# Output stores of whole 128-row tiles in a linear-attention and SwiGLU kernel on one Trainium2 core

## The chip, the cores and the metric

The kernel runs on one core of one Trainium2 chip. Its time is the device time of an execution in microseconds (us). Five engines work side by side, each through its own list of instructions: PE multiplies matrices, DVE and ACT work on vectors and read PE's results from PSUM, POOL and SP mostly issue transfers here. The data are moved by the 16 DMA engines of the core. An instruction waits on semaphores for what it needs, and everything behind it in the same list waits with it.

## The reference

The kernel computes a linear attention and feeds its result to a feed-forward block. The part that matters, cut:

```
q, k, v: [8, 8, 576, 64]          # batch, heads, positions, head size
phi(x) = concat(relu(x) * cos(theta), relu(x) * sin(theta))   # theta = pi/2 * position / 576
kv  = einsum('bhsf,bhsd->bhfd', phi(k), v);  z = sum over s of phi(k)
num = einsum('bhsf,bhfd->bhsd', phi(q), kv)
den = einsum('bhsf,bhf->bhs', phi(q), z) + 1e-6
x   = (num / den) transposed to [8 * 576, 8 * 64]             # 4608 tokens of 512
g   = x @ w_gate;  val = x @ w_val                            # [512, 1536] each
out = (g * sigmoid(g) * val) @ w_out                          # [4608, 512] in float32
```

The output has 4608 x 512 float32 values, 9.4 MB.

## The kernel before, in words

**Tiles.** The positions of a batch are dealt to partitions so that position p of 64 partitions holds 9 tokens in a row: `out_v = out.rearrange("(b p c) f -> b c p f", p=SH, c=NC)` with SH = 64 and NC = 9. So there are 8 x 9 = 72 chunks of 64 tokens; the tokens of a chunk lie 9 rows apart in the output. A tile is two chunks in order, 128 partitions: chunk 2t on partitions 0 to 63, chunk 2t + 1 on 64 to 127. There are 36 tiles. Where 2t is the last chunk of a batch (2t % 9 is 8), the tile straddles two batches. Four tiles (512 tokens) are a token group, tg 0 to 8.

**Stages.** The attention of a batch makes its tiles of x, SP transposes them with DMA (L749 writes xT; L852 transposes the features phi(q), named phit, for the products L789). The matmuls of gate and value (L990), and of the output (L1155), are done for most groups with seven products of half-size blocks in place of eight (a Winograd scheme); the sums that these need are made by DVE (L963 for xT, L1106 for the hidden values). Group 0, and a part of group 1, use plain matmuls (L917, L1065, L1275). In `out_jobs` the four blocks of a group's output are called e11, e12, e21 and e22: first or second pair of tiles, first or second 256 columns. They are evicted from the PSUM banks to a buffer `ob` by ACT (L632) and DVE (L636, L1212). In the last group the pieces are evicted tile by tile, into memory that r_q had held, so the profile shows them as r_q.

**Stores.** `store_jobs` (L1118) stores a tile as two transfers of 64 rows of 512 columns (L1124): from POOL for groups 1 to 6, from SP for group 0 and for group 7's first two tiles. The last group has stores of its own: `store_two_jobs` (L1248) stores 64 rows of two tiles and 256 columns in one transfer, the first half of the rows from SP, the second from ACT (L1253); `store_tile_jobs` (L1258) does the same for one tile (L1262).

**The order of the work.** Each piece of work is a job with the engines that can do it, the jobs that it comes after, and the rooms (PSUM banks, a pair of `ob`) that it gets and puts back. The jobs are numbered as they are made, and written out in an order given by a table of numbers, ORDER, with the room that a job takes behind a colon. Times in the Job calls (`tail`, `dma`, the number beside the engine) are estimates for a planner that made such a table; with a table given they change nothing in the program.

Of the kernel before, what the change touches and what calls it, by code (L numbers as in the profile page):

```python
# [18 lines left out]
def kernel(  # L19
# [10 lines left out]
    nc = tc.nc  # L30
# [4 lines left out]
    SH = 64  # L35
    NC = S // SH
# [1081 lines left out]
    def store_jobs(t, after, put, queues, cols=slice(0, d_model)):  # L1118
        for e in range(2):
            q_ = queues[e]  # L1120

            def fn(j, e=e):
                idx = 2 * t + e
                {"POOL": nc.gpsimd, "SP": nc.sync, "ACT": nc.scalar}[j.eng].dma_start(  # L1124
                    out=out_v[idx // NC, idx % NC][:, cols], in_=ob_of(t)[e * SH:(e + 1) * SH, cols])
            Job({q_: 535 if q_ == "POOL" else 610}, fn, after=after, put=put, tail=1500.0, dma=(1450.0, 480.0))
# [3 lines left out]
    def ob_of(t):  # L1130
        return pair_of(t // 2)[:, t % 2]

    def pair_of(p):
        return (ob_last if obs[p].kind == "last ob" else ob_all)[:, obs[p].at[0]]

    def out_jobs(tg, key):
# [68 lines left out]
        if last:  # L1205
            store_two_jobs(t0, slice(0, HD), [e11], ("SP", "ACT"))
# [7 lines left out]
        if last:  # L1214
            store_two_jobs(t0 + 2, slice(HD, d_model), e22, ("SP", "ACT"))
# [6 lines left out]
        if last:  # L1222
            for n in range(2):
                store_tile_jobs(t0 + 2, n, slice(0, HD), [e21[n]])
        else:
            for t in (t0 + 2, t0 + 3):
                store_jobs(t, e22 + e21, [rooms[1]], ("POOL", "POOL"))
# [8 lines left out]
        if last:  # L1236
            for n in range(2):
                store_tile_jobs(t0, n, slice(HD, d_model), [e12[n]])
        else:
            for t in (t0, t0 + 1):  # L1240
                store_jobs(t, [e11] + e12, [rooms[0]], ("SP", "SP") if tg == NTG - 2 else ("POOL", "POOL"))
# [5 lines left out]

    def store_two_jobs(t, cols, after, queues):  # L1248
        for e in range(2):
            def fn(j, e=e):  # L1250
                (b, c), (b1, _) = divmod(2 * t + e, NC), divmod(2 * t + 2 + e, NC)
                assert b == b1
                {"SP": nc.sync, "ACT": nc.scalar}[j.eng].dma_start(  # L1253
                    out=out_v[b, c:c + 3:2, :, cols].rearrange("c p f -> p c f"),
                    in_=pair_of(t // 2)[e * SH:(e + 1) * SH, :, cols])
            Job({queues[e]: 660}, fn, after=after, tail=1300.0, dma=(700.0, 560.0))

    def store_tile_jobs(t, i, cols, after, queues=("SP", "ACT")):  # L1258
        for e in range(2):
            def fn(j, e=e):  # L1260
                b, c = divmod(2 * (t + i) + e, NC)
                {"SP": nc.sync, "ACT": nc.scalar}[j.eng].dma_start(  # L1262
                    out=out_v[b, c][:, cols], in_=pair_of(t // 2)[e * SH:(e + 1) * SH, i, cols])
            Job({queues[e]: 620}, fn, after=after, tail=1300.0, dma=(700.0, 280.0))
# [36 lines left out]
    for lo, hi in ((0, 2), (2, 4)):  # L1301
        def fn(j, lo=lo, hi=hi):
            o = raws[1, "k"][:, lo:hi]
            relu_on(j.eng, o, o)
# [118 lines left out]
    for tg in range(1, NTG):  # L1423
# [43 lines left out]
        6:7 4:6 12:1 8:0 10:5 16:3 20:4 29 5:8 9:7 13:0 17:1 1:3 376 7 187 28 191 11 186 188 189 31 30 24:7 18:2 26:3  # L1467
        22:6 21:6 25:2 33 32 2:7 67:0 34:45 14:1 70a 36a 35a 38a 37a 3 27 380 19 68v 69 15 23 71 0 41:2 44 40:0 43
        72:340 84:7 78:561 39:1 42 73 74 75:3 85a 79 86 80 87v 81:2 88 76:3 77 45 101:7 89:560 95:341 47 90 96 377
        102a 378 91 92:3 97 48 82:5 93:6 55:1 83 94 98:0 192 193 109 190 103 110 113 381 114 46 99:1 51:3 52 49  # L1470
# [105 lines left out]
```

## Time and profile before

| | before |
|---|---|
| median of 3 runs (lowest to highest) | 299.13 us (298.21 to 299.59) |
| the profiled execution's own time | 298.66 us |
| span of the profiled execution | 296.8 us |
| mean granted clock of PE | 0.996 |
| PE busy, matmuls | 290.1 us (98%), 3292 |
| DVE, ACT, POOL busy | 252.9, 199.1, 69.1 us |
| bytes moved by the DMA queues | 40.90 MB, 138 GB/s |
| stores from POOL, SP, ACT | 52, 18, 6 |

The span goes from the first instruction to the last; the time is taken around it, 1.86 us more in the profiled execution. The stores from SP are 12 halves of 128 KB (8 for group 0, 4 for group 7), and in the last group 2 of two tiles and 4 of one; those from ACT are 2 and 4 of the last group. Instructions that issue a transfer are marked SPq, ACTq and POOLq, and are not counted as busy time. A line "DMA packets" counts the packets of all transfers by size; a store of 64 rows of 512 columns has 64 packets of 2 KB, one of 256 columns packets of 1 KB. The chain is followed back from the last instruction, at each step to what released it.

### The profile page before, as it was taken

The page shows a single profiled execution, that of the slowest core. Times are in us where ns is not written, and L with a number is a line of the kernel's source. Part 1 is how long each engine was busy: PE and PEld are TensorE (multiplying, and loading weights), DVE is VectorE, ACT ScalarE, POOL GpSimd, SP SyncE. Part 2 cuts the span into 40 slices and gives each one's busy share as a digit, 9 for nine tenths or more (in the row PEclk, how much of TensorE's full clock was granted, in tenths as well). Part 3 has the DMA queues.
Part 4 walks back from the last instruction along what each step waited for, and adds up shares of the span by engine and source line. Part 5 has one row for each costly group of instructions (what it writes and reads, how often), then busy time and mean ns, then how long its engine had stood idle before and what let it go on. Part 6 is the DMA issues. An engine that isn't in the chain of part 4 may idle for free.

```text
span 296.8 us, 8157 instructions
## 1 busy us (share of the span) xinstructions
PE 290.1 (98%) x3292; PEld 237.7 (80%) x3292; DVE 252.9 (85%) x513; ACT 199.1 (67%) x423; POOL 69.1 (23%) x122
## 2 busy tenths in 40 slices
PE   8999999999999999999999999999999999999993
PEld 4697455665877888988898898888988898888882
DVE  7976889889987899999898977998778968968882
ACT  6664347978479868985499689976566555564630
POOL 7963530012015012213343020400050032002000
PEclk9999999999999999999999999999999999999998
DMA  7999999999969999599959947980270036000226
GB/s 255 232 196 198 202 206 209 229 202 155 170 149 171 199 209 144 102 172 148 209 118 159 197 68 131 208 146 2 38 171 8 2 89 127 0 2 18 55 53 161
DMA packets 71973, 40.90 MB, mean 138 GB/s; under 512 B 48768, under 2 KB 68736, under 8 KB 71936
## 3 DMA queue, kind: packets, MB, share of 16 engines
q0 software_dynamic: 24800, 24.39, 49.9%
q1 hardware_dynamic: 46528, 15.47, 27.6%
q10 hardware_dynamic: 608, 0.52, 0.6%
q8 instruction: 26, 0.43, 0.6%
q14 instruction: 11, 0.09, 0.1%
HBM read 37.75 MB, written 9.44 MB: 159 GB/s over the span
## 4 chain that ended last, share of the span: by engine, by line
PE 87%; DMA 9%; DVE 2%; issue 0%; DVEq 0%
PE banks L990 43%; PE banks L1155 23%; DMA xT<-x 4%; DMA phit<-r_q 4%; PE banks L440 4%; PE banks L917 4%; PE banks L1275 3%; PE banks L789 3%; PE banks L718 2%; PE banks L1065 2%; DMA wo_sb<-in_v_dram 1%; DVE v L292 1%; PE banks L371 1%; PE banks L784 1%; PE banks L1323 0%; PE banks L314 0%
## 5 line engine op out<-in xcount | busy, mean ns | idle before, releaser
L1124 POOL DMA_DIRECT2D out_dram<-ob x52 | 27.3, 532 | 128.4 <-ACT ob L632 87.6
L630 ACT COPY banks<-banks 128x512 f32<-128x512 f32 (+1 forms) x53 | 30.4, 577 | 22.3 <-PE banks L990 9.9
L1049 ACT ACTIVATE sg<-banks 128x512 bf16<-128x512 f32 x72 | 40.9, 599 | 5.8 <-PE banks L990 5.6
L1085 DVE TENSOR_TENSOR ht<-sg,banks 128x512 f16<-128x512 bf16 x60 | 40.4, 682 | 4.8 <-PE banks L990 4.4
L1155 PEld LDWEIGHTS <-ht 128*128 128x128 f16 x384 | 37.5, 98 | 4.5
L990 PEld LDWEIGHTS <-wg_sb 128*128 128x128 f16 x384 | 36.7, 98 | 5.3
L990 PEld LDWEIGHTS <-wgs_sb 128*128 128x128 f16 x368 | 35.4, 98 | 6.4 <-issue 0.5
L1010 DVE TENSOR_TENSOR banks<-m,banks 128x512 f32<-128x512 f32 x44 | 30.2, 692 | 7.3 <-PE banks L990 6.0
L990 PEld LDWEIGHTS <-wv_sb 128*128 128x128 f16 x320 | 31.2, 98 | 3.7
L990 PE MATMUL banks<-kvt,wgs_sb 128*128 128x256 f16 x236 | 33.8, 273 | 0.3 <-DVE kvt L963 0.3
L1155 PEld LDWEIGHTS <-sums 128*128 128x128 f16 x288 | 28.0, 98 | 3.4
L630 ACT COPY m<-banks 128x512 f32<-128x512 f32 x44 | 25.5, 590 | 5.7 <-PE banks L990 5.7
L990 PE MATMUL banks<-xT,wg_sb 128*128 128x256 f16 x192 | 28.6, 273 | 0.0
L632 ACT ACTIVATE ob<-banks 128x512 f32<-128x512 f32 x32 | 19.1, 596 | 10.6 <-PE banks L1155 9.3
L1155 PE MATMUL banks<-wo_sb,ht 128*128 128x256 f16 x192 | 25.2, 273 | 0.0
L990 PE MATMUL banks<-kvt,wg_sb 128*128 128x256 f16 x168 | 24.4, 273 | 0.0
L1155 PE MATMUL banks<-wt_sb,sums 128*128 128x256 f16 x192 | 24.2, 273 | 0.0
L820 DVE TENSOR_TENSOR x<-banks,rec 128x512 f16<-128x512 f32 x31 | 21.3, 690 | 3.1 <-PE banks L990 0.5
L990 PE MATMUL banks<-xT,wv_sb 128*128 128x256 f16 x160 | 23.8, 273 | 0.0
L1155 PE MATMUL banks<-wt_sb,ht 128*128 128x256 f16 x192 | 22.8, 272 | 0.0
L890 ACT ACTIVATE r_q<-raw_q,tanq 128x256 bf16<-128x256 bf16 x45 | 20.1, 507 | 0.0
L292 DVE TENSOR_TENSOR v<-raw_kv,tab 128x1152 bf16<-128x1152 bf16 x27 | 19.9, 750 | 0.0
(160 smaller groups left out, 540.1 us busy)
## 6 DMA issues: line engine op xcount, KB each, us to landing
out_dram<-ob POOLq DMA_DIRECT2D x52, 128.0 KB, 3.3
raw_kv<-in_k_dram POOLq DMA_DIRECT2D x7, 576.0 KB, 6.2
raw_q<-in_q_dram POOLq DMA_DIRECT2D x12, 288.0 KB, 9.9
raw_kv<-in_v_dram POOLq DMA_DIRECT2D x6, 576.0 KB, 9.3
out_dram<-ob SPq DMA_DIRECT2D x12, 128.0 KB, 2.8
wg_sb<-in_moe_w_gate_dram POOLq DMA_DIRECT2D x5, 256.0 KB, 9.0
wv_sb<-in_moe_w_val_dram POOLq DMA_DIRECT2D x5, 256.0 KB, 9.6
wo_sb<-in_v_dram SPq DMA_DIRECT2D x2, 576.0 KB, 4.1
```

The costliest lines, as they stand in the source:

```text
L292: nc.vector.tensor_tensor(out=v2s[b == 1][:, g, :, :, 0:D], in0=(first if b == 0 and g == 0 else {"v": raw_of(b, "v")})["v"][:, g].unsquee ...
L440: nc.tensor.matmul(out=st["f", tg, fc, lo][i], lhsT=(wg_sb, wv_sb)[i][:, kc, fs], rhs=xT[tg][:, ts, kc], start=(kc == 0), stop=(kc == KC - 1))
L630: nc.scalar.copy(out=out, in_=in_)
L632: nc.scalar.mul(out=out, in_=in_, mul=mul)
L820: tt(out=x_.rearrange("p (i y d) -> p i y d" if pairs else "p (y e d) -> p e y d", d=D, **({"i": 2} if pairs else {"e": 2})), in0=view()[: ...
L890: nc.scalar.activation(out=home()[:, :, c, 1], in_=raws[b, "q"][:, :, c], func=AF.Relu, scale=tanq[:, c:c + 1])
L990: nc.tensor.matmul(out=to[:, i], lhsT=a[:, c, 2 * u + i], rhs=x()[:, :, c], start=first and i == 0 and c == 0, stop=c == KH - 1, skip_grou ...
L1010: tt(out=bank(c), in0=one(m7_all, m).rearrange("p i x -> p (i x)"), in1=bank(b), op=ALU.add)
L1049: nc.scalar.activation(out=gates(rooms[w])[:, :, jh * HT:(jh + 1) * HT], in_=src, func=AF.Silu, scale=DOWN)
L1085: tt(out=ht[:, 4 * u + w:4 * u + w + 3:2, jh * HT:(jh + 1) * HT], in0=gates(rooms[w])[:, :, jh * HT:(jh + 1) * HT], in1=src.rearrange("p ( ...
L1124: {"POOL": nc.gpsimd, "SP": nc.sync, "ACT": nc.scalar}[j.eng].dma_start(out=out_v[idx // NC, idx % NC][:, cols], in_=ob_of(t)[e * SH:(e + ...
L1155: nc.tensor.matmul(out=to, lhsT=a[:, kc, i * P:(i + 1) * P], rhs=b[:, kc], start=first and kc == 0 and i == 0, stop=kc == HC - 1, skip_gro ...
```

## The change

A tile that does not straddle two batches is stored by one transfer of its 128 rows, `whole_tile_job`: in DRAM the two chunks `out_v[b, c:c + 2]`, in SBUF the 128 partitions of `ob_of(t)`. That holds for groups 1 to 7, where one engine issues both halves. Straddling tiles, and group 0, keep two transfers of 64 rows. In the last group each of the eight pieces of 128 rows and 256 columns (e11, e22, e21 and e12, two tiles each) is one transfer; SP has the first tile's of each, ACT the second's. A piece of e22 is stored when its own eviction is done, where both were waited for. The table ORDER is another, with 1425 jobs instead of 1453, and lines move by some places (L1155 is L1165 after the change, L1198 is L1208, L1212 is L1223, L1275 is L1269, L1323 is L1317; L1124 becomes L1126 for halves and L1134 for whole tiles).

```
     def store_jobs(t, after, put, queues, cols=slice(0, d_model)):
+        if len(queues) == 1 and 2 * t % NC < NC - 1:
+            return whole_tile_job(t, cols, after, queues[0], put, 6500.0)
         for e in range(2):
-            q_ = queues[e]
+            q_ = queues[e % len(queues)]
...
-            Job({q_: 535 if q_ == "POOL" else 610}, fn, after=after, put=put, tail=1500.0, dma=(1450.0, 480.0))
+            Job({q_: 560}, fn, after=after, put=put, tail=6500.0, dma=(1270.0, 480.0))
+
+    def whole_tile_job(t, cols, after, queue, put=(), tail=1300.0):
+
+        def fn(j):
+            b, c = divmod(2 * t, NC)
+            {"POOL": nc.gpsimd, "SP": nc.sync, "ACT": nc.scalar}[j.eng].dma_start(
+                out=out_v[b, c:c + 2][:, :, cols], in_=ob_of(t)[:, cols])
+        Job({queue: 600}, fn, after=after, put=list(put), tail=tail, dma=(700.0, 560.0))
...
         if last:
-            store_two_jobs(t0, slice(0, HD), [e11], ("SP", "ACT"))
+            for n in range(2):
+                whole_tile_job(t0 + n, slice(0, HD), [e11], ("SP", "ACT")[n])
...
         if last:
-            store_two_jobs(t0 + 2, slice(HD, d_model), e22, ("SP", "ACT"))
+            for n in range(2):
+                whole_tile_job(t0 + 2 + n, slice(HD, d_model), e22[n:n + 1], ("SP", "ACT")[n])
...
-                store_tile_jobs(t0 + 2, n, slice(0, HD), [e21[n]])
+                whole_tile_job(t0 + 2 + n, slice(0, HD), [e21[n]], ("SP", "ACT")[n])
...
-                store_jobs(t, e22 + e21, [rooms[1]], ("POOL", "POOL"))
+                store_jobs(t, e22 + e21, [rooms[1]], ("POOL",))
...
-                store_tile_jobs(t0, n, slice(HD, d_model), [e12[n]])
+                whole_tile_job(t0 + n, slice(HD, d_model), [e12[n]], ("SP", "ACT")[n])
...
-                store_jobs(t, [e11] + e12, [rooms[0]], ("SP", "SP") if tg == NTG - 2 else ("POOL", "POOL"))
+                store_jobs(t, [e11] + e12, [rooms[0]], ("SP",) if tg == NTG - 2 else ("POOL",))
...
-        6:7 4:6 12:1 8:0 10:5 16:3 20:4 29 5:8 9:7 13:0 17:1 1:3 376 7 187 28 191 11 186 188 189 31 30 24:7 18:2 26:3
...
+        8:2 4:4 12:1 10:0 14:3 24:7 20:6 16:5 5:2 9:0 13:1 29 21:5 25:3 17:4 0 373 28 374 375 11 191 15 6:1 26:0 22:7
...
```

What stands at the end of SP's list, before (-) and after (+); `2x64x512` is a whole tile, two chunks of 64 rows in DRAM:

```order
 L749 DMA_TRANSPOSE xT<-x 128x4x128 x8
-L1124 DMA out_dram<-ob 64x512 x3
-L1253 DMA out_dram<-r_q 64x2x256
-L1124 DMA out_dram<-ob 64x512
-L1253 DMA out_dram<-r_q 64x2x256
-L1262 DMA out_dram<-r_q 64x256 x4
-L1571 UNCONDITIONAL_BRANCH
+L1134 DMA out_dram<-ob 2x64x512 x2
+L1134 DMA out_dram<-r_q 2x64x256 x4
+L1563 UNCONDITIONAL_BRANCH
```

Ten stores have become six, and group 7's two tiles stand ahead of all stores of the last group.

The end of ACT's list, where the last group's values are gated (L1049 makes the gate's sigmoid, sg) and the outputs evicted, before:

```order
L1049 ACTIVATE sg<-banks 128x2x256 x3
L630 COPY banks<-banks 128x256 x2
L632 ACTIVATE ob<-banks 128x2x256
L632 ACTIVATE r_q<-banks 128x2x256 x2
L1253 DMA out_dram<-r_q 64x2x256 x2
L1262 DMA out_dram<-r_q 64x256 x4
```

and after:

```order
L1049 ACTIVATE sg<-banks 128x2x256 x3
L632 ACTIVATE ob<-banks 128x2x256
L630 COPY banks<-banks 128x256 x2
L632 ACTIVATE r_q<-banks 128x2x256 x2
L1134 DMA out_dram<-r_q 2x64x256 x4
```

Six issues have become four. The eviction of group 7's last block (L632 to ob) has moved ahead of two copies; on PE the product that it evicts stands 8 matmuls earlier than before. ACT's four stores are of e22, e11, e21 and e12, in this order; SP's of e11, e22, e21 and e12.

The end of POOL's list, where groups 3 to 6 had one run of 28 halves:

```order
-L1124 DMA out_dram<-ob 64x512 x28
-L1571 UNCONDITIONAL_BRANCH
-L1571 ISA
+L1134 DMA out_dram<-ob 2x64x512 x7
+L1126 DMA out_dram<-ob 64x512 x2
+L1134 DMA out_dram<-ob 2x64x512 x5
+L1126 DMA out_dram<-ob 64x512 x2
+L1563 UNCONDITIONAL_BRANCH
+L1563 ISA
```

The pairs of halves are tiles that straddle two batches. In the whole list 52 halves have become 22 whole tiles and 8 halves.

DVE's list around the sums of xT (L963, into kvt) for the first group whose gate and value are done with seven products. L292 weighs k and v with the table of cosines and sines, L1106 sums hidden values, L1198 and L1212 (now L1208 and L1223) add up output blocks. Before:

```order
L1106 TENSOR_TENSOR sums<-ht,sums 128x512
L1106 TENSOR_TENSOR sums<-ht,sums 128x1024
L963 TENSOR_TENSOR kvt<-xT 128x512 x2
L963 TENSOR_TENSOR kvt<-xT,kvt 128x512
L1198 SCALAR_TENSOR_TENSOR banks<-ob,banks 128x512
L292 TENSOR_TENSOR v_0_186<-raw_kv,tab 128x18x64
```

and after:

```order
L292 TENSOR_TENSOR v_0_186<-raw_kv,tab 128x18x64
L1208 SCALAR_TENSOR_TENSOR banks<-ob,banks 128x512
L292 TENSOR_TENSOR v_0_186<-raw_kv,tab 128x18x64
L963 TENSOR_TENSOR kvt<-xT 128x512 x2
L963 TENSOR_TENSOR kvt<-xT,kvt 128x512
L292 TENSOR_TENSOR v_0_186<-raw_kv,tab 128x18x64
```

An addition for the output and one of the weighings now stand ahead of the sums of xT, and two sums of hidden values (L1106) that stood ahead come later.

More of the change, by code (lines that the diff above doesn't have):

```diff
@@ L1246, in out_jobs @@
         J_["ht_free", tg, 1, 1] = P4 + ts[1]
[L1248 to L1264, printed above, removed]
     def plain_out_jobs(key):
@@ L1466 @@
     ORDER = """
-        6:7 4:6 12:1 8:0 10:5 16:3 20:4 29 5:8 9:7 13:0 17:1 1:3 376 7 187 28 191 11 186 188 189 31 30 24:7 18:2 26:3
-        22:6 21:6 25:2 33 32 2:7 67:0 34:45 14:1 70a 36a 35a 38a 37a 3 27 380 19 68v 69 15 23 71 0 41:2 44 40:0 43
-        72:340 84:7 78:561 39:1 42 73 74 75:3 85a 79 86 80 87v 81:2 88 76:3 77 45 101:7 89:560 95:341 47 90 96 377
-        102a 378 91 92:3 97 48 82:5 93:6 55:1 83 94 98:0 192 193 109 190 103 110 113 381 114 46 99:1 51:3 52 49
[63 rows of a table removed]
+        8:2 4:4 12:1 10:0 14:3 24:7 20:6 16:5 5:2 9:0 13:1 29 21:5 25:3 17:4 0 373 28 374 375 11 191 15 6:1 26:0 22:7
+        67:4 68a 70a 31 30 33 32 186 7 1:6 27 69 23 377 187 34:23 41:4 44 18:0 71 19 35a 37a 36a 38a 72:670 78:121
+        84:0 40:5 73 79 87a 85a 74 80 75:0 81:1 86 39:3 43 76:6 2:7 89:010 101:2 42 90 102a 3 88 91 92:3 188 45 93:2
[62 rows of a table added]
     """
```

125 rows, old and new, of the table ORDER are left out of this document.

## The prediction

> **What bounds the kernel now.** I read the engine line of the page first, then the chain that ended last, then the table by stage, and last the end of the span instruction by instruction.
>
> ```profile
> span 296.8 us, 8157 instructions
> PE 290.1 (98%) x3292; PEld 237.7 (80%) x3292; DVE 252.9 (85%) x513; ACT 199.1 (67%) x423; POOL 69.1 (23%) x122
> PE 87%; DMA 9%; DVE 2%; issue 0%; DVEq 0%
> ```
>
> PE is busy for 98% of the span and makes 87% of the chain. The change leaves the 3292 matmuls as they are. So a store matters only where it keeps PE waiting, or after PE's last matmul. The table by stage says how much of both there is; its columns are the stretch, then busy time of each engine in it, the granted clock, the DMA engines' share and GB/s.
>
> ```profile
> core 0: us, PE busy (x) PEld busy (x) DVE busy (x) ACT busy (x) POOL busy (x), PEclk, DMA share, GB/s
> 18.00:60.00 42.00, 42.00 (x460) 26.93 (x458) 34.67 (x82) 26.44 (x60) 12.18 (x18) 1.00 1.30 209
> 60.00:70.00 10.00, 9.68 (x147) 6.46 (x145) 8.88 (x17) 7.70 (x20) 2.92 (x5) 1.00 0.95 163
> 70.00:85.00 15.00, 14.66 (x115) 10.97 (x114) 13.92 (x26) 9.14 (x19) 0.00 (x0) 1.00 1.26 203
> 85.00:270.00 185.00, 185.00 (x2135) 163.37 (x2133) 161.77 (x308) 134.86 (x287) 37.05 (x69) 1.00 0.65 114
> 292.00:296.80 4.80, 0.00 (x0) 0.00 (x0) 0.31 (x1) 0.00 (x0) 0.00 (x0) 0.78 0.60 156
> ```
>
> Between 18 and 270 us PE loses 0.32 us in the third row and 0.34 us in the fourth, and nothing in the others. The last 4.8 us hold no matmul: the stores' tail. The two waits and what leads to them:
>
> ```profile
> PE banks L990 <- DVE kvt L963: 0.3, 1, 0.3
> PE banks L789 <- DMA phit<-r_q: 0.3, 1, 0.3
> ...
> 53.56 11.17 DMA phit<-r_q
> ...
> 69.92 12.09 DMA xT<-x
> ```
>
> Both come from a transpose by DMA that SP issues. So an early PE wait hangs on how soon DMA work lands, and that is the place where stores could hurt or help in the middle.
>
> **The change, part by part.** *The middle.* 52 stores on POOL become 22 whole ones and 8 halves.
>
> ```profile
> L1124 POOL DMA_DIRECT2D out_dram<-ob x52 | 27.3, 532 | 128.4 <-ACT ob L632 87.6
> ```
>
> That takes 52 − 30 = 22 issues of 0.53 us from POOL, 11.7 us in all. POOL is busy for 23% and PE never waits for it, so this is worth nothing. The rewritten order moves the sums of xT (L963) behind other DVE work and the 8 matmuls of L789 ahead by about 1.4 us; both waits may go (−0.7) or change places. I take −0.3, with ends −0.7 and +0.5 from the sizes of these two waits. I price a POOL store of another shape below.
>
> *The tail.* Here the rows by instruction (start, duration, engine, operation, idle before):
>
> ```profile
> 280.77 1.47 PE L1155 MATMUL banks<-wo_sb,sums 128*128 128x256 f16 x12
> ...
> 284.03 0.63 ACT L630 COPY banks<-banks 128x256 f32<-128x256 f32 x2 [3.28 <-PE banks L1155]
> 284.56 0.62 ACT L632 ACTIVATE ob<-banks 128x512 f32<-128x512 f32 x1
> 285.20 1.76 SPq L1124 DMA_DIRECT2D out_dram<-ob  x3
> ...
> 290.38 1.47 PE L1155 MATMUL banks<-wo_sb,sums 128*128 128x256 f16 x12
> 291.24 3.17 SPq L1262 DMA_DIRECT2D out_dram<-r_q  x4
> 291.25 2.82 ACTq L1262 DMA_DIRECT2D out_dram<-r_q  x4
> 291.89 0.42 DVE L636 TENSOR_SCALAR r_q<-banks 128x256 f32<-128x256 f32 x1 [0.23 <-PE banks L1155]
> ...
> L1262 SPq DMA_DIRECT2D out_dram<-r_q x4: 467/546/550, 291.2 to 293.9; - x4
> ```
>
> The last result is ready at 292.31 us; SP's last issue ends at 294.41, because each queue has four of them in a row, which take 0.7 to 0.8 us each with the gaps between them (3.17 / 4, 2.82 / 4). The last of SP's starts at 293.86 (the last row) and lands 2.0 us later, at 295.86; the span ends 0.94 us after that. The change leaves SP six stores and ACT four where there were 10 and 6. It also starts group 7's last two stores earlier: their product stands 8 matmuls earlier on PE (8 × 1.47 / 12 = 1.0 us), so it ends at 282.24 − 1.0 = 281.3, and its eviction (0.62 us) now stands ahead of the two copies of 284.03, so the first store can be issued at about 282.0 instead of 285.2.
>
> *The shape of the new transfer.* This is the term that decides, and no row of before has it. What the rows do have:
>
> ```profile
> DMA packets 1537, 1.59 MB, mean 122 GB/s; under 512 B 256, under 2 KB 1280, under 8 KB 1536
> q1 hardware_dynamic: 928, 1.05, 33.6%
> q10 hardware_dynamic: 608, 0.52, 13.7%
> out_dram<-ob SPq DMA_DIRECT2D x4, 128.0 KB, 2.4
> out_dram<-r_q SPq DMA_DIRECT2D x2, 128.0 KB, 3.3
> out_dram<-r_q ACTq DMA_DIRECT2D x2, 128.0 KB, 3.9
> out_dram<-r_q SPq DMA_DIRECT2D x4, 64.0 KB, 2.0
> ```
>
> This is the stretch from 284 to 297 us: 16 stores, and 256 packets under 512 B, 16 for each store beside its data: one from each of the 16 DMA engines. Every one of these stores begins with the same count on both sides, 64 rows in DRAM against 64 partitions, and 16 divides 64. The whole-tile store begins with 2 (chunks) in DRAM and 128 (partitions) in SBUF. If the work is dealt to the engines by this outermost count, two engines carry all of it, and fourteen stand idle; if it is dealt by rows or packets, nothing changes. The store of 64 x 2 x 256, which has an inner dimension that the SBUF side walks too, was dealt in the same way as the plain one, so the inner dimensions don't upset the dealing; the outer ones are equal in every row, and can't tell the two apart. [...] The 16 small packets for counts of 64 agree with both.
>
> The price on two engines. Each of them carries half of two stores of 256 KB (64 packets of 2 KB from each) and of eight of 128 KB (64 of 1 KB from each): 128 packets of 2 KB and 512 of 1 KB. On ACT's queue 13.7% of 16 engines over 13 us is 28.5 us for 512 packets of 1 KB and 96 small ones: 47 ns each if the small ones cost the same, 56 if they cost nothing; I take the middle, 51. For 2 KB there is the stretch from 285.5 to 288.6 us with three stores:
>
> ```profile
> DMA packets 240, 0.39 MB, mean 127 GB/s; under 512 B 48, under 2 KB 48, under 8 KB 240
> q1 hardware_dynamic: 240, 0.39, 55.4%
> GB/s 0 0 0 0 0 0 0 0 0 0 106 185 264 211 159 264 159 238 106 212 238 264 159 291 132 264 106 212 185 317 106 317 106 344 79 53 0 0 0 0
> ```
>
> 55.4% × 16 × 3.1 us is 27.5 us for 192 packets and 48 small ones: 114 to 143 ns; I take 114, since two engines do not have fourteen others writing beside them. Sum: 128 × 0.114 + 512 × 0.051 = 40.7 us on each of the two. The cheap end is 14.6 + 512 × 0.047 = 38.6; the dear one 18.3 + 512 × 0.068 = 53.1, the 68 ns being SP's queue (33.6% × 16 × 13 / 1.05 MB, by KB). The first bytes are in the eleventh of the 40 slices, 286.3, and follow the issue at 285.20 by 1.1 us, so here they start at 283.1. The end: 283.1 + 40.7 = 323.8, and 0.94 us to the span's end as now: 324.8. Against 296.8 that is +28.0; with −0.3 from the middle +27.7.
>
> *POOL's stores of that shape.* Two engines would hold 64 × 114 to 143 ns, or 7 to 9 us, of one store. The landing of now:
>
> ```profile
> out_dram<-ob POOLq DMA_DIRECT2D x52, 128.0 KB, 3.3
> ```
>
> So each would land some 6 us later, and loads with packets on these two engines up to 9 us later. Between 85 and 270 us the DMA engines work at 114 GB/s and PE never waits, and the first POOL stores come after the two waits. Hidden by loads that are issued well ahead; without that cover up to 0.3 us a wait for some ten loads, +3. I take nothing.
>
> The profiled run took 298.66 us for its span of 296.8, and stands 0.47 under the median of 299.13. 299.13 + 27.7 gives **326.8 us**.
>
> **Rivals.** *A: dealt over 16 engines as now, the change helps or does nothing.* For it: 256 KB in one transfer is the same number of packets of the same size, and the small packets show 16 engines with every store. It decides from about eight engines on, where the tail's 1.5 MB would take 40.7 / 4 = 10 us from 283.1, hidden under the compute that ends at 292.3. Then SP's last store is issued right behind the last result, at 292.4, and lands as SP's 128 KB stores do, 2.4 to 3.3 us from its start: 294.8 to 295.7, against 295.86. With 0.94 behind it that is −0.2 to −1.0, with the middle −0.5 to −1.3; I take −0.9: 298.2 us. Against it: the unequal outer counts.
>
> *B: ACT becomes late.* ACT's first store now waits for the second half of e22 and three others queue behind it. If a store of 128 rows over 16 engines takes twice the 0.7 us of one of 64 to issue, ACT issues four in 4 × 1.42 = 5.7 us from 290.4, waits for nothing else, and the last lands from 294.6 with 3.9 us at 298.5: 2.6 us later than now, 301.7 us. Against it: of SP's 0.8 us a store the issue itself took 0.55 (the row of L1262), so a part of the 0.7 is waiting, not work that grows with the rows.
>
> *C: SP's and ACT's transfers fall on different pairs.* Then SP's pair carries 128 packets of 2 KB and 256 of 1 KB, 14.6 + 13.1 = 27.7 us from 283.1, end 311.7, +14.9: 314.0 us. Nothing in the trace speaks for or against.
>
> **How the numbers follow.** Two engines for the new shape: 0.68, of which one shared pair (the likeliest, 326.8; own range 324 to 339 from the cheap and the dear price) 0.58 and C 0.10. A: 0.28, of which 0.10 beyond 0.5% (1.5 us, about what a measurement of this kernel can tell from no change) and 0.18 within it. B 0.04. So faster 0.10, same 0.18, slower 0.72. The range goes from 297.6, where A is within half a per cent, to 336, which leaves out A's better part and the dearest prices.
>
> **What would show it.** Right: after 292 us a stretch of 25 us or more with DMA alone, its share at about 2/16, the two queues' packets the same in size and number but for fewer small ones; landings of 20 us and more for the last stores; PE ending near 291.5 and the two waits about as they are. Wrong: landings of 2 to 4 us and a DMA share near 0.6 at the end (A); four issues of ACT that follow each other after 292.3 (B); a PE that waits in the middle, with the landings of POOL's stores at 10 us or more, would show that the cover assumed there was not.

## The result, and the profile after

The median of four runs of the changed kernel is 379.83 us (374.41 to 383.98), against 299.04 before. Two of these four runs, and one of the four of e2_pool_whole below, lie more than 1.5% above the fastest run of the same kernel; they are left out of the comparisons, which go by 376.96 us for the changed kernel. That is 1.261 times as long, 95% interval 1.246 to 1.276. The forecast was 326.8. Its direction held and its size didn't: +28 forecast, +78 measured.

The page of the profiled execution (374.41 us of its own, span 372.6):

```profile
span 372.6 us, 8116 instructions
PE 305.3 (82%) x3292; PEld 244.7 (66%) x3292; DVE 252.9 (68%) x511; ACT 200.8 (54%) x425; POOL 63.5 (17%) x100
```

The same 3292 matmuls were busy for 305.3 us instead of 290.1, and PE's share fell from 98% to 82%. The table by stage, cut where PE ends. Before:

```profile
core 0: us, PE busy (x) PEld busy (x) DVE busy (x) ACT busy (x) POOL busy (x), PEclk, DMA share, GB/s
85.00:291.90 206.90, 206.85 (x2333) 182.67 (x2330) 179.44 (x342) 144.52 (x306) 39.13 (x73) 1.00 0.61 109
291.90:296.80 4.90, 0.00 (x0) 0.00 (x0) 0.41 (x1) 0.00 (x0) 0.00 (x0) 0.79 0.61 158
```

and after:

```profile
85.00:345.40 260.40, 221.44 (x2328) 188.67 (x2326) 181.45 (x342) 144.95 (x305) 33.69 (x51) 0.90 0.73 84
345.40:372.60 27.20, 0.00 (x0) 0.00 (x0) 0.43 (x1) 0.00 (x0) 0.00 (x0) 0.59 0.13 46
```

Up to 85 us little has changed (PE is busy for 83.9 us of it, 83.2 before: the two early waits of 0.3 us are gone). From there to PE's end it takes 260.4 us instead of 206.9, **+53.5**; behind PE's end 27.2 instead of 4.9, **+22.3**. Together that is the 75.8 us between the spans. In the middle, 39.0 us are PE idle (260.40 − 221.44) and 14.6 are PE busy for longer (221.44 − 206.85) at a granted clock of 0.90 where it was 1.00.

What PE waited for in the changed kernel:

```profile
PE banks L990 <- DMA xT<-x: 19.7, 3, 8.0
PE banks L990 <- DVE banks L1010: 9.6, 2, 8.2
PE banks L990 <- DVE kvt L963: 6.0, 1, 6.0
PE banks L990 <- ACT banks L630: 3.3, 1, 3.3
```

Six groups lose 5 to 8 us each at their first products of gate and value, the first of them in two pieces (3.3 and 1.4 us). What DVE waited for shows the cause where PE waited for DVE:

```profile
DVE kvt L963 <- DMA xT<-x: 26.9, 4, 8.7
DVE raw_kv L963 <- DMA xT<-x: 9.6, 1, 9.6
DVE v L292 <- DMA raw_kv<-in_v_dram: 7.6, 1, 7.6
```

In five groups it is xT: either PE's own products read it, or PE stands behind the sums of xT, which DVE makes late. The 8.2 us under L1010 are of this kind too, since that work follows a sum of xT on DVE that waited 8.67 us. In the first group it is two loads. POOL issued the loads of k and v at 89.75 and 90.55 us, between whole-tile stores. They landed after 14.2 and 18.5 us, where the kernel before has 6.1 and 9.8:

```profile
raw_kv<-in_k_dram POOLq DMA_DIRECT2D x1, 576.0 KB, 14.2
raw_kv<-in_v_dram POOLq DMA_DIRECT2D x1, 576.0 KB, 18.5
```

ACT waited for the one and DVE for the other, and PE lost 4.7 us behind them. One place with xT as an example, POOL, SP and PE of the changed kernel:

```profile
208.55 1.65 POOL L1134 DMA_DIRECT2D out_dram<-ob  x2 [12.00 <-ACT ob L632]
211.19 1.58 POOL L1134 DMA_DIRECT2D out_dram<-ob  x2 [0.99 <-ACT ob L632]
...
208.66 11.54 SPq L749 DMA_TRANSPOSE xT<-x  x4
...
227.01 1.01 PE L990 MATMUL banks<-xT,wg_sb 128*128 128x256 f16 x4 [6.04 <-DVE kvt L963]
```

Four stores of POOL and four transposes of SP go out in the same 12 us, the transposes land late, and PE stands for 6.04 us. Not only the landing is late: at another place phit's transpose held SP's queue for 16.4 us from 134.75 (6.7 us in the kernel before), so three transposes to xT went out only from 151.2 us on, and PE stood for 8.0 us until 154.66. In the example, the first four matmuls behind the wait take 1.01 us where four took 0.60. The granted clock around it:

```profile
221.00:227.00 6.00, 0.00 (x0) 0.02 (x1) 0.53 (x2) 1.28 (x3) 0.00 (x0) 0.73 1.45 141
227.00:232.00 5.00, 4.99 (x30) 3.82 (x31) 4.51 (x9) 1.68 (x3) 0.00 (x0) 0.64 0.83 188
232.00:237.00 5.00, 5.00 (x108) 4.33 (x107) 4.27 (x10) 2.17 (x5) 0.00 (x0) 1.00 0.01 3
```

In the 5 us behind the wait it is 0.64, then 1.00 again. Taken by single microseconds, it is 1.00 in the wait up to 223 us, 0.89 in the next one, 0.50 from 224 to 230, 0.70 from 230 to 231 and 1.00 from 231 on. The 5 us lose 1.8 us (0.36 of 5), so this wait of 6.04 us costs about 8.

The end, from 336 us on, by DMA packets (q1 is SP's queue, q10 ACT's):

```profile
GB/s 0 9 22 22 40 49 51 69 49 54 49 54 49 49 51 47 49 47 49 47 49 48 48 49 47 49 47 49 47 49 49 47 49 47 49 47 49 47 9 0
DMA packets 1301, 1.59 MB, mean 43 GB/s; under 512 B 20, under 2 KB 1044, under 8 KB 1300
q1 hardware_dynamic: 780, 1.05, 8.1%
q10 hardware_dynamic: 520, 0.52, 4.0%
```

There are ten stores and 20 small packets, two for each, where it was 16 for each; together the queues hold 12.1% of sixteen engines, about two; and the rate is flat at 48 GB/s. That is the end that was forecast.

The stores of POOL, the whole tiles and the eight halves of straddling tiles, whose form is the old one:

```profile
out_dram<-ob POOLq DMA_DIRECT2D x22, 256.0 KB, 14.2
out_dram<-ob POOLq DMA_DIRECT2D x8, 128.0 KB, 15.1
```

Before, all 52 landed with a median of 3.3 us. So the old form is as late as the new one where it is issued behind it. POOL's last whole tile can be seen nearly alone: from 332 to 335 us of the changed kernel, POOL's queue (q0) moves 53 GB/s and holds 13.4% of sixteen engines:

```profile
q0 software_dynamic: 45, 0.16, 13.4%
```

That is two engines here too.

### The profile page after: what moved, and what is told of

It reads as the page before. It is cut to its first block, busy times and chain, and to the rows that moved or that the text cites. A ratio compares the mean times of both kernels' runs of the same rounds, so it can differ in the third digit from the quotient of the medians.

```text
span 372.6 us, 8116 instructions
## 1 busy us (share of the span) xinstructions
PE 305.3 (82%) x3292; PEld 244.7 (66%) x3292; DVE 252.9 (68%) x511; ACT 200.8 (54%) x425; POOL 63.5 (17%) x100
## 3 DMA queue, kind: packets, MB, share of 16 engines
q0 software_dynamic: 34304, 24.46, 47.8%
## 5 line engine op out<-in xcount | busy, mean ns | idle before, releaser
L990 PE MATMUL banks<-xT,wg_sb 128*128 128x256 f16 x192 | 30.9, 287 | 25.8 <-DMA xT<-x 19.7
L1049 ACT ACTIVATE sg<-banks 128x512 bf16<-128x512 f32 x72 | 42.2, 594 | 15.0 <-PE banks L990 14.8
L1085 DVE TENSOR_TENSOR ht<-sg,banks 128x512 f16<-128x512 bf16 x60 | 40.5, 682 | 12.1 <-PE banks L990 10.0
L1134 POOL DMA_DIRECT2D out_dram<-ob x22 | 17.9, 815 | 168.1 <-ACT ob L632 75.5
L990 PEld LDWEIGHTS <-wgs_sb 128*128 128x128 f16 x368 | 37.2, 102 | 10.8 <-issue 4.1
L990 PEld LDWEIGHTS <-wv_sb 128*128 128x128 f16 x320 | 33.5, 105 | 16.0 <-issue 10.0
L1165 PEld LDWEIGHTS <-ht 128*128 128x128 f16 x384 | 37.7, 99 | 5.3
L990 PE MATMUL banks<-kvt,wgs_sb 128*128 128x256 f16 x236 | 37.0, 287 | 3.3 <-ACT banks L630 3.3
L1010 DVE TENSOR_TENSOR banks<-m,banks 128x512 f32<-128x512 f32 x44 | 30.3, 692 | 7.9 <-PE banks L990 3.5
L990 PE MATMUL banks<-kvt,wv_sb 128*128 128x256 f16 x136 | 24.3, 315 | 9.6 <-DVE banks L1010 9.6
L1165 PEld LDWEIGHTS <-sums 128*128 128x128 f16 x288 | 28.4, 99 | 3.6
L1165 PE MATMUL banks<-wt_sb,sums 128*128 128x256 f16 x192 | 26.1, 279 | 0.0
L1165 PE MATMUL banks<-wo_sb,ht 128*128 128x256 f16 x192 | 25.8, 278 | 0.0
L292 DVE TENSOR_TENSOR v<-raw_kv,tab 128x1152 bf16<-128x1152 bf16 x27 | 20.0, 751 | 7.6 <-DMA raw_kv<-in_v_dram 7.6
L1049 ACT ACTIVATE sg<-m 128x512 bf16<-128x512 f32 x24 | 15.1, 629 | 18.5 <-DVE ht L1085 9.9
L632 ACT ACTIVATE ob<-banks 128x512 f32<-128x512 f32 x32 | 19.0, 597 | 10.4 <-PE banks L1165 10.3
L963 DVE TENSOR_TENSOR kvt<-xT 128x512 f16<-128x512 f16 x14 | 5.7, 420 | 27.4 <-DMA xT<-x 26.9
## 6 DMA issues: line engine op xcount, KB each, us to landing
out_dram<-ob POOLq DMA_DIRECT2D x22, 256.0 KB, 14.2
```

Of the source, the lines that this page charges most:

```text
L292: nc.vector.tensor_tensor(out=v2s[b == 1][:, g, :, :, 0:D], in0=(first if b == 0 and g == 0 else {"v": raw_of(b, "v")})["v"][:, g].unsquee ...
L632: nc.scalar.mul(out=out, in_=in_, mul=mul)
L963: engine(j).tensor_tensor(out=xs_of(tg)[:, n - 1], in0=x(), in1=y(), op=ALU.subtract)
L990: nc.tensor.matmul(out=to[:, i], lhsT=a[:, c, 2 * u + i], rhs=x()[:, :, c], start=first and i == 0 and c == 0, stop=c == KH - 1, skip_grou ...
L1010: tt(out=bank(c), in0=one(m7_all, m).rearrange("p i x -> p (i x)"), in1=bank(b), op=ALU.add)
L1049: nc.scalar.activation(out=gates(rooms[w])[:, :, jh * HT:(jh + 1) * HT], in_=src, func=AF.Silu, scale=DOWN)
```

## The experiments

Two theories stood at first. *Two engines*: a store whose outer counts are 2 and 128 is carried by 2 of the 16 DMA engines, and everything follows from that. *Order*: the rewritten order makes PE wait for xT, whatever the stores are. All kernels from e1 to e9 keep the order of the changed kernel (e5 moves POOL's stores in it).

**e1_halves.** Only the form of the stores goes back:

```
-            {...}[j.eng].dma_start(out=out_v[b, c:c + 2][:, :, cols], in_=ob_of(t)[:, cols])
+            for e in range(2):
+                {...}[j.eng].dma_start(out=out_v[b, c + e][:, cols], in_=ob_of(t)[e * SH:(e + 1) * SH, cols])
```

> The changed kernel with its own order of the work, but every whole tile is stored as two transfers of 64 rows again, one behind the other from the same queue. Two engines (a store whose outer counts are 2 and 128 is carried by 2 of the 16 DMA engines, and this alone costs): 297.5 to 300.5 us, PE without waits of over 1 us after 10 us, 16 small packets for each store. Order (the rewritten order makes PE wait): over 345 us, with the 6 to 8 us waits for xT still there.

Measured: 302.48 us, 1.012 of the kernel before (1.009 to 1.014). Some 74 of the 78 us are the stores' form. The other 3.5 us or so are the order and the number of stores at the end; the first theory, with 300.5 at most, missed that. PE waits once for xT,

```profile
PE banks L990 <- DMA xT<-x: 1.6, 1, 1.6
```

at 139 us, its busy time in this execution is 1.65 us longer than before's, and its last matmul ends at 294.5 instead of 291.9. Behind that come 6.8 us instead of 4.9; each queue now has eight stores of the last group's halves, where the kernel before had six.

**e2_pool_whole** and **e3_end_whole** split the stores: whole tiles from POOL alone, and from SP and ACT alone. The edit is e1's with a condition on `j.eng == "POOL"`.

> The changed kernel, whole tiles from POOL only (22 stores of groups 1 to 6); the stores of SP and ACT at the end are halves of 64 rows. Two engines: the waits for xT stay (about 39 us of PE waits and some 15 us by a lower clock), PE ends near 345, the end takes 4 to 6 us behind it: 348 to 362 us. If the loss in the middle came back from the end's stores, which it can't precede, or from the order: not below 375 or near 299.

> The changed kernel, whole tiles from SP and ACT only (group 7's two tiles and the eight pieces of the last group); POOL stores halves. Two engines: PE ends near 292 as in the kernel before, the two engines then carry 768 KB each until about 34 us after the first store's issue: 320 to 328 us. Order: over 345.

Measured: 357.4 us (356.14 to 358.39) and 323.46 (322.24 to 326.12), both as expected. Over e1 that is +54.9 and +21.0; added to e1's 302.48 they make 378.4, against 376.96 for the changed kernel, whose runs spread wider than the difference. The two losses are separate and add up. What waits in e2:

```profile
PE banks L990 <- DMA xT<-x: 29.5, 4, 11.9
PE banks L990 <- DVE banks L1010: 10.2, 2, 8.5
PE banks L990 <- ACT banks L630: 3.1, 1, 3.1
```

The landing of SP's transposes to xT (L749, min, median, max), in e1 and then in e2:

```profile
DMA to landing us min/median/max: 2.9/5.0/12.7
```

```profile
DMA to landing us min/median/max: 2.5/11.7/16.2
```

The median went up by 6.7 us, and PE's waits are 43 us over six groups; the five that wait for xT lose 38 us, 7.6 each (the 8.5 us under L1010 stand behind a sum of xT again). So there was hardly any slack between a transpose's landing and its use.

**e4_rows62.** Is it the count, or the 128 rows, or the size? Here the halves have 62 rows (two rows of each 64 are left out of the output).

```
-                ...dma_start(out=out_v[b, c + e][:, cols], in_=ob_of(t)[e * SH:(e + 1) * SH, cols])
+                ...dma_start(out=out_v[b, c + e][0:62, cols], in_=ob_of(t)[e * SH:e * SH + 62, cols])
```

> As e1_halves, but each half stores 62 of its 64 rows (the last two rows of 64 are left out of the output, apart from those of group 0 and of straddling tiles). No transfer has an outer count of 2 or 128 partitions; the largest divisor of 62 up to 16 is 2. Two engines by the largest common divisor: 2 small packets for each of the 12 stores at the end, a tail of 20 us or more behind PE, and if POOL deals its stores in the same way the waits for xT as well: 365 to 385 us; with POOL's stores over all engines 318 to 328. An outer count of 2 in DRAM, or 128 rows in one transfer, as such: 296 to 300.5 us.

Measured: 322.03 us (321.79 to 322.43). Its end, from 284 us on:

```profile
GB/s 0 18 27 39 34 48 32 41 64 48 52 50 50 51 49 49 48 48 49 48 48 48 49 48 49 48 48 49 48 48 48 49 48 49 47 49 48 42 7 0
DMA packets 1281, 1.54 MB, mean 43 GB/s; under 512 B 40, under 2 KB 1032, under 8 KB 1280
```

There are 20 stores (the expectation's 12 was a miscount) and 40 small packets: two engines each, and again 48 GB/s, with no outer 2 and no 128 rows in one transfer. So the stores of SP and ACT follow the largest divisor, up to 16, that the outer counts have in common: 16 small packets each with 64 against 64 (320 for 20 stores in e1), two with 2 against 128, two with 62 against 62. One thing the runs leave open: in all of them the smaller outer count divides the larger, so the words "in common" are not tested apart. POOL's stores of 62 rows behaved otherwise: no wait for xT beyond e1's 1.6 us, and landings (L1136)

```profile
DMA to landing us min/median/max: 2.1/3.4/9.1
```

as in the kernel before. From 276.0 to 277.5 us, with the last of them and two halves of 64 rows in flight, POOL's queue holds 86% of sixteen engines; with the whole tile it held 13.4%.

**e7_rows57** and **e8_rows61** are e4 with other counts.

> As e4_rows62 with 57 rows of 64 stored (seven left out). The largest divisor of 57 up to 16 is 3. Each engine then carries 19 rows of a half where it carried 32 on two engines: 768 x 19 / 32 = 456 KB at the 43.4 ns per KB of the changed kernel's tail are 19.8 us from 285.5, so the last lands near 305: 306 to 311 us, with 3 small packets for each store of SP and ACT at the end. If what counts is that the rows aren't 64 or that some are left out: near 302 or as e4_rows62, 322.

> As e4_rows62 with 61 rows of 64 stored. 61 is a prime over 16: one engine. It carries 768 x 61 / 32 = 1464 KB at 43.4 ns per KB, 63.5 us from 285.5: 345 to 356 us, one small packet for each store. If two engines were the least that a store gets: 318 to 323 us.

Measured: 311.04 us (two runs, 310.17 and 311.9) and 352.39 (351.77 and 353.02). e7, from 284 to 309 us:

```profile
GB/s 0 0 0 26 43 39 43 56 75 72 72 79 102 79 75 70 74 70 66 70 70 74 72 70 74 72 70 72 74 70 72 72 72 72 70 64 15 0 0 0
DMA packets 1201, 1.42 MB, mean 57 GB/s; under 512 B 60, under 2 KB 972, under 8 KB 1200
```

e8, from 284 to 350:

```profile
GB/s 0 10 14 26 36 25 26 25 25 26 24 25 26 26 25 25 24 24 24 24 24 24 24 24 24 24 24 24 24 24 24 24 24 24 24 24 24 24 24 1
DMA packets 1241, 1.52 MB, mean 23 GB/s; under 512 B 20, under 2 KB 996, under 8 KB 1240
```

Three small packets for each of the 20 stores at 57 rows, one at 61; 72 and 24 GB/s, so 24 GB/s for each engine that takes part, with one, two or three. Both times are in or within 0.1 us of the expected range. In e8, SP's and ACT's stores together make 24 GB/s: both queues deal to the same engine. That settles rival C of the prediction, two pairs: it is one.

**e6_one_whole.** Why is the middle so dear? The author's theory, the collision: the transposes to xT have packets on the engines that the slow stores keep busy, and land late for it. Then few stores should cost nearly as much as many. Here one tile of each group 1 to 6 is stored whole, the others as halves; the condition stands in e1's edit.

```
+            if t in (5, 9, 12, 17, 21, 25):
```

> As e2_pool_whole, but in each of the groups 1 to 6 only one tile is stored whole, the third or second last that the group stores (6 whole stores in place of 22); the others are halves. [...] Collision: the waits stay for the most part, 325 to 352 us. Cost in proportion to the stores' number (55.4 us times 6/22 above the 302.5 of e1_halves): 312 to 320 us.

Measured: 333.89 us (331.62 to 334.33), +31.4 over e1, and 57% of e2's loss with 27% of its stores. The transposes to xT land with a median of 9.3 us:

```profile
DMA to landing us min/median/max: 2.5/9.3/13.0
```

One slow store for each group is enough to make them late. That speaks for the collision and against a cost by number.

**e5_held.** The whole stores of POOL are held back until the transposes that they met have landed (the edit, cut).

```
...
+                for i in range(OUT):
+                    nc.gpsimd.tensor_copy(out=hold2, in_=xT_of(OUT * (tg + 2) + i)[0:1, 0, 0:2])
+                for t, b, c in J_.get(("held", tg), []):
+                    nc.gpsimd.dma_start(out=out_v[b, c:c + 2], in_=ob_of(t))
```

> As e2_pool_whole, but POOL issues the whole-tile stores of a group later: it first reads an element of each of the four xT tiles of the group after next (four copies of two elements), whose transposes run at the time at which the stores were issued, and issues them behind that. The stores are the same. Collision (the slow stores cost because the transposes to xT have packets on the stores' engines, and PE waits for them): PE's waits in the middle fall from 42 us to under 10, 303 to 318 us. Traffic (stores on two engines cost wherever they stand): over 340 us.

Measured: 357.52 us (354.79 to 359.25), as slow as e2. By the number this is the other theory's range (over 340), and the forecast of 303 to 318 was missed. But the waits are others now:

```profile
PE banks L990 <- DVE banks L1010: 15.1, 1, 15.1
PE banks L789 <- ACT kv L630: 13.3, 1, 13.3
PE banks L990 <- ACT sg L1049: 12.1, 1, 12.1
PE banks L990 <- ACT ob L632: 5.3, 1, 5.3
```

No wait of PE for xT is left, and the transposes to xT land with a median of 2.6 us:

```profile
DMA to landing us min/median/max: 2.4/2.6/13.0
```

So the collision with these transposes was there, and is gone. The loss went elsewhere. ACT waits for `ob` to be stored before it can evict the next group's output into it:

```profile
ACT ob L632 <- DMA out_dram<-ob: 43.9, 3, 17.1
```

and three of PE's four waits above are for ACT. The fourth is for DVE, which waits up to 15.8 us for ACT there. The held stores now meet phit's transposes, which land up to 27.5 us after their issue (13.2 at most in e1). Stores that take 9 to 24 us to land, with a group about every 30 us in the kernel before, have found no place here where nothing waits for them; on this the theory of traffic was right.

**e9_pairs.** Two tiles in two transfers, as the change meant it, but with 64 on the outside: half the partitions of both tiles.

```
+                eng.dma_start(out=out_v[b, c:c + 3:2, :, cols].rearrange("c p f -> p c f"),
+                              in_=pair_of(p0 // 2)[e * SH:(e + 1) * SH, :, cols])
```

> The changed kernel's order; where the two tiles of a pair lie in one batch, one transfer stores 64 partitions of both tiles (64 rows by 2 tiles by 512 columns, 256 KB as the whole tile has, outer counts 64 and 64), so two transfers for two tiles as with whole tiles; other tiles, and the last group's single pieces, are two halves. Two engines: the size doesn't matter, the outer count does: as e1_halves, 300 to 303 us, and the 256 KB stores of POOL land in 3 to 9 us where the whole tiles' took 14. If 256 KB in one transfer is what costs: over 340.

Measured: 302.21 us, 1.011 (1.009 to 1.014), as e1. These transfers (L1140; 16 of 256 KB and two of 128) land in 2.5 to 4.6 us:

```profile
DMA to landing us min/median/max: 2.5/3.5/4.6
```

where the whole tile's 256 KB from POOL took 8.8 to 17.5, median 14.2. The size is innocent. That fewer transfers save POOL issues is true, 38 in place of e1's 52, and gains nothing that can be measured here.

**e10, e11 and e12** try the end of the kernel before, where SP's and ACT's issues queue behind the last results. e10 hands two of the last stores to POOL, e11 and e12 hand it group 7's.

```
e10  -                store_tile_jobs(t0, n, slice(HD, d_model), [e12[n]])
e10  +                store_tile_jobs(t0, n, slice(HD, d_model), [e12[n]], ("SP", "ACT") if n else ("POOL", "POOL"))
e11  -    ... ("SP", "SP") if tg == NTG - 2 else ("POOL", "POOL"))
e11  +    ... ("POOL", "POOL"))
e12  +    ... ("POOL", "SP") if tg == NTG - 2 else ("POOL", "POOL"))
```

> The kernel before with one change at its end: the two halves of the last group's second last piece (e12 of the first tile) are issued by POOL, which has nothing left to do then, in place of SP and ACT. SP and ACT then have three stores each behind 291 us in place of four and issue the last piece at 292.4 where SP issued its last at 293.86: the last lands near 294.9, 1 us earlier: 297.7 to 298.6 us with the kernel before at 299.1. If POOL's stores land late or the span's end hangs on something else: 298.8 to 299.8.

> The kernel before with group 7's last four halves issued by POOL, as the groups before it have it, in place of SP. SP's list at the end is then two stores of two tiles and four of one tile. POOL's drain took 7 us behind its last issue (274.86 to 281.84 in the kernel before, to 300.05 in e10_end_pool, where it ended the span), so behind an issue at 287 it ends near 294 and is hidden. If SP's queue is what makes the last stores late: the last lands near 294.9, 1 us earlier, 297.7 to 298.7 us. If ACT's stores or the waits on earlier stores are: 298.8 to 299.5. If the drain comes out longer: above 300.

> The same with two of the four on POOL (the first half of each tile) and two on SP: in SP's list one store less stands between the last group's. If SP's queue is what makes the last stores late, part of the gain of e11_pool4: 298.0 to 299.0 us. Otherwise 298.8 to 299.5.

Measured: e10 302.27 us, 1.011 (1.008 to 1.013), a miss. SP's last store starts at 293.52 and lands 2.73 us later, at 296.25, but POOL's closing instruction runs until 300.05 (the longest of the three drains, 6903 ns from 293.1):

```profile
L1571 POOLq DRAIN  x3: 51/93/6903, 293.1 to 300.6; - x3
```

e11 and e12: 298.63 and 298.53 us against 298.99 for the kernel before in the same series, ratios 0.9993 (0.9978 to 1.0008) and 0.9987 (0.9974 to 1.0000). Both medians lie in the range that was expected if SP's queue is what makes the last stores late, but the gains of 0.4 and 0.5 us can't be told from none, so this stays open. In e11 SP is free of group 7's stores, but its two stores of two tiles still hold it, like ACT, until 291.3:

```profile
288.81 2.44 SPq L1253 DMA_DIRECT2D out_dram<-r_q  x2
288.81 2.43 ACTq L1253 DMA_DIRECT2D out_dram<-r_q  x2
291.34 2.79 ACTq L1262 DMA_DIRECT2D out_dram<-r_q  x4
291.34 2.49 SPq L1262 DMA_DIRECT2D out_dram<-r_q  x4
```

Why the second issue takes 1.3 us there wasn't tried. No kernel of these beats the one before by more than its measurement can tell.

## Why the prediction was wrong in size

- **The shape of the new transfer: right.** Two engines, one pair for SP and ACT together, a flat rate and a share of 2/16 at the end, two small packets for each store. No row of before showed two engines, nor that both queues share them; both were the author's estimate. The changed kernel showed 2 small packets a store, 12.1% of sixteen engines and 48 GB/s for both queues together. In e4, e7 and e8 the small packets went with the divisor of the rows (2 for 62, 3 for 57, 1 for 61); in e9 256 KB in one transfer landed in 2.5 to 4.6 us, so it isn't the size.
- **The tail: right in mechanism, sized a quarter too high.** +28.0 forecast, +22.3 measured. The 1.57 MB went at 48 GB/s, 33 us, where 51 and 114 ns a packet made it 40.7. The packet times came from stretches in which sixteen engines were at work; with one, two or three at work, each makes 24 GB/s (24 in e8, 48 in the changed kernel, 72 in e7), 43 ns for 1 KB.
- **POOL's stores of that shape: this step failed, and with it the forecast.** It said: "each would land some 6 us later, and loads with packets on these two engines up to 9 us later", and "Hidden by loads that are issued well ahead ... I take nothing", with +3 if that cover were missing. The measured cost is 55 us (e2 over e1). The delay itself was in part well sized: transposes 6.7 us later in the median and two loads 8 and 9 us later, but the stores 11 us (14.2 against 3.3) and not 6. What failed is the cover. Those that wait on the engines are not only loads: the transposes to xT are issued when x is ready, land 4.1 us later in the median of the kernel before, and their readers stand ready. The cover of the loads was too thin as well, in the first group. The price without the cover was wrong too: 0.3 us a wait is the size of a wait of the kernel before, not of the delay of up to 9 us that the prediction had just worked out. In its place stand 5 to 8 us for each of six groups, 39 us in all, and some 15 us of longer matmuls at a lower clock behind them, for which the forecast had no term. The prediction had shown, two parts earlier, that PE's only waits between 18 and 270 us hang on DMA transposes, but it did not ask how much slack the other groups had. The last of its signs of being wrong, a PE that waits in the middle with POOL's stores landing at 10 us or more, is what came. e6 and e5 show that it is this collision; the one other place for such stores that was tried, in e5, was no better.
- **The middle by the order: wrong, though small.** −0.3 taken, +0.5 as the far end. The two early waits did go (0.65 us), but e1 shows PE's end 2.6 us later: a new wait of 1.6 us for xT at 139 us, and 1.65 us more of busy time. Why the busy time grew isn't known; that execution of e1 was the slowest of four, and in e4, with the same order and the same wait, it grew by 0.5 us. As for the wait, three of that group's four transposes stand behind phit's on SP, which holds the queue for 7.6 us from 126.9 (6.7 us from 126.4 in the kernel before), so they go out at 134.6 to 137.7 instead of 133.2 to 136.1. The first of them also takes 6.0 us to land in place of 3.8; it lands at 140.6, and PE stands from 139.1 on. Which of the moved jobs makes the difference wasn't tried.
- **Rival A: refuted** (it needed eight engines or more). **Rival B: did not come.** ACT's last two issues did take 5.5 and 5.3 us, as long as SP's, but the two DMA engines wrote all the while at a flat rate, so these engines set the end; over sixteen engines (e1) an issue of ACT took 0.5 to 0.6 us. **Rival C: refuted** by 48 GB/s with both queues.

## What to carry to other kernels

Before two transfers are made one, look at the outermost count of both sides: in these runs, on SP's and ACT's queues, the number of DMA engines that carried a transfer, by its small packets, was their largest common divisor up to 16, not the number of partitions (2 against 128 got 2, 62 rows got 2, 57 got 3, 61 got 1, 64 all 16). From POOL, 2 against 128 got two engines as well (13.4% of sixteen), while 57, 61 and 62 rows cost nothing in the middle (the first store of group 7 left SP at 285.4, 285.1 and 284.4 us, at 285.6 in e1). The cheap sign in a trace of SP's and ACT's stores is the number of small packets for each transfer. And a slow transfer is priced by every transfer that lands later because of it, here the transposes that feed the bound engine: the delay less the slack that each of them has, not the bytes or the mean share of the queue.

## What the runs showed of the hardware that was not expected

- POOL's stores of 62 and 61 rows landed as those of 64 did (2.1 to 9.1 us and 2.1 to 9.6 us, both with a median of 3.4; 2.2 to 9.0 and 3.4 for the stores of 64 from ob in e1), but the whole tile, 2 against 128, did not (8.8 to 17.5 us). For each whole tile its queue shows 432 packets more than for two halves: 34304 packets in the changed kernel against 24800, 9504 more for 22 tiles. What these small packets add to the lateness of the transposes wasn't tried by itself. The trace makes them the lesser part: for the whole tile that e6 stores at 237.46 us, the 448 smallest of them take 3.7 us, summed over all engines, while the data hold two engines for about 5 us each (128 KB at 26 GB/s, half of the 53 above).
- POOL's closing drain, which follows its last issue, is long: 6.9 us in e10, where it ended the span, 7.8 us from 274.1 in the kernel before and 7.2 us from 287.0 in e11, in both of which it was hidden.
- In the changed kernel the stores on two engines held the issuing queue as well: the last stores of SP and ACT took 5.3 to 5.5 us each to issue, and SP's four transposes to xT took 11.5 us at 208.66 where they took 9.0 before, gaps included.
